# Seven block products for eight in the first 256 features of x @ w_in, from token group 4 on, with shared sums copied inside PSUM

## The chip, the cores and the metric

One core of one Trainium2 chip. The metric is the device time of one execution of the whole program, in microseconds (us). The engines are TensorE (matmuls; PE in the profile, its weight loads PEld), VectorE (DVE), ScalarE (ACT), GpSimd (POOL) and SyncE (SP, here a queue of DMAs).

## What is computed

An mLSTM cell over 4 batches, 8 heads, 768 steps and 40 dimensions per head; its output, as 3072 tokens of 320 features, goes through a two-layer block with a "tanh shrink" between.

```python
for t in range(S):                       # S = 768
    m_new = np.maximum(f_gate[:, :, t] + m, i_gate[:, :, t])
    f_stab, i_stab = np.exp(f_gate[:, :, t] + m - m_new), np.exp(i_gate[:, :, t] - m_new)
    C = f_stab * C + i_stab * einsum('bhd,bhe->bhde', vt, kt)
    n = f_stab * n + i_stab * kt
    y[:, :, t] = sigmoid(o_gate) * einsum(C, qt) / max(|n.qt|, 1)
x = y as [3072, 320]
h = x @ w_in                             # [3072, 2048]
g = h - np.tanh(h)
out = g @ w_out                          # [3072, 320]
```

All products are in f32; TensorE makes two passes (two loads, two matmuls) of each.

## The kernel before

The cell works in 24 units of 128 tokens (`n` in the code). Two units make a token group `g` of 256 tokens, so there are 12. The 2048 hidden features are cut in 8 pairs `p` of two blocks of 128. An *item* is one group with two pairs. Its up products fill two PSUM banks `ph_up` (128 hidden features x 2 pairs x 256 tokens each, one bank for each block of a pair). ScalarE squares them (`z`), with the row sums accumulated, and squares again (`q`); VectorE makes `gt` = c z h (the "cube") and then `gt` = (q + c') gt (the "last" step). That is the polynomial for h - tanh(h).

The down product with `w_out` is made in seven block products for eight (a Strassen-Winograd form). For it VectorE makes sums of `gt` (`s`, `s1` to `s4`) and, once, of `w_out` (`wT`); 14 products of 128x160 an item are accumulated over a whole group in three banks `pS0`, `pS1`, `pS2`, the first two with the tags `po0` and `po1`. After the last item of a group `put_together` copies a part `a` out of `pS0` (ScalarE) and makes the output `ob` from the three banks with four VectorE operations; ScalarE issues its DMA. The next group takes the same banks.

Up to 212 us a planner (a list scheduler with costs and ranks) orders units 0 to 11 and the groups 0 to 3. After that comes the main loop, which this case is about: 32 items, four for each of the groups 4 to 11, here numbered #0 (from 212.09 us) to #31. Iteration x makes the up products of item x and, since `LAG` is 1, the down products of item x-1. `merge` writes out each iteration's TensorE steps in order (the list `dense`) and puts other work between by a clock of estimated costs: `Clock.later(key, wait, step)` holds a step back for a time, and `Clock.need(key)` issues at once whatever a key still holds. Instructions on an engine run in the order in which they are written (the classes `Pinned` and `T` keep it). The cell work of units 12 to 23 is spread over the main loop: an even item has crossed scores `ps` (then `P` on VectorE), an odd one outputs and state (`pT`, `pc`, then `zt`, `yt`, state on VectorE). Items #24 to #31 have little or none. A unit's output `ys` is turned into feature rows through DRAM (`yt`, `y_rows`) and lands in `xT` by SP's DMAs.

An item's up products are eight of 128 features x 256 tokens (two pairs, two blocks, two chunks of 128 input features) and, for the remaining 64 features, eight "quarter" products (`rest`) that run in a quarter of the array each. The main loop's body before is

```python
dense, rest = up(some, shrink(x), bool(scored or new[:1]))
dense.append((..., lambda: halves(rest, *(crossed_scores(n) for n in new[:1]))))
...
dense += down_seven(some)                # of item x-1: all 14 products
```

Of the kernel before, what the change touches and what calls it, by code (L numbers as in the profile page):

```python
# [49 lines left out]
FP = mybir.dt.float32  # L50
# [29 lines left out]
def kernel(  # L80
# [195 lines left out]
    FROM = (0, 128, DM - 128)  # L276
    NK = 2
    HALF = 64
    assert FROM[1] + HALF == FROM[2]
# [41 lines left out]
    w_out = const.tile([128, NFF, DM], FP, name="w_out")  # L321


    xT = [const.tile([128, NK + 1, TG], FP, name=f"xT{i}") for i in range(NX)]

# [24 lines left out]
    def load_unit(n, names=("kz", "qz", "v", "k", "o", "q2"), queue=SP, behind=(), crossed=False):  # L350
        c, b = divmod(n, B)
        t = ld.setdefault(n, {})
        t["crossed"] = crossed
        for name in names:
            if crossed and (name == "v" or name == "k" and n + B < NU):
                whole = load.tile([L, H if name == "v" else WIDE, D], FP, name=name, tag=name, bufs=3)
                t[name] = whole
                if name == "k":
                    G.memset(whole[:, H:], 0.0)
                load_crossed(whole[:, 0:H], (v if name == "v" else k)[b, c])  # L360
            elif name in ("kz", "qz"):
                t[name] = load.tile([128, HH, L], FP, name=name, tag=name, bufs=3)
                for i in range(2):
                    src = kT if name == "kz" else qT
                    dma = queue.dma_start(out=t[name][i * HALF:i * HALF + D], in_=src[b, c, :, i * HH:(i + 1) * HH])
                    if behind:
                        tc.add_manual_dep(dma.ins, behind[-1].ins.name, SYNC, reason="order of transfers")
            elif name == "k":
                if n + B < NU:
                    t["k"] = load.tile([L, WIDE, D], FP, name="k", tag="k", bufs=3)  # L370
                    queue.dma_start(out=t["k"].rearrange("p h d -> p (h d)"),
                                    in_=bass.AP(k.tensor, k[b, c].offset, [[H * D, L], [1, WIDE * D]]))
            elif name != "q2":
                src, bufs = {"v": (v, 3), "o": (o_gate, 4)}[name]
                t[name] = load.tile([L, H, D], FP, name=name, tag=name, bufs=bufs)
                queue.dma_start(out=t[name], in_=src[b, c])
            elif c:
                t["q2"] = load.tile([TOP, len(TRIOS), L], FP, name="q2", tag="q2", bufs=3)
                for i in range(TRIO):
                    queue.dma_start(out=t["q2"][i * D:(i + 1) * D, 0:len(range(i, H, TRIO))], in_=qT[b, c, :, slice(i, H, TRIO)])  # L380
# [50 lines left out]
    NS = NG * NP + 2  # L431
# [160 lines left out]
    def blocks_of(p):  # L592

        def slices(a, n):
            return slice(a * 128, (a + n) * 128)

        every, whole = slice(0, 128), [(slice(0, 128), slices(0, 2), moe_w_in[0:128, slices(2 * p, 2)])]
        odd = moe_w_in[FROM[1]:FROM[1] + 128, slices(2 * p + 1, 1)]
        both = bass.AP(odd.tensor, odd.offset, [[DFF, 128], [(FROM[2] - FROM[1]) * DFF - 128, 2], [1, 128]])
        whole.append((every, slices(2, 2), both))  # L600
        half = (FROM[1], FROM[2] + HALF)
        for i in range(2):
            whole.append((slice(i * HALF, (i + 1) * HALF), slices(4, 1), moe_w_in[half[i]:half[i] + HALF, slices(2 * p + i, 1)]))
# [7 lines left out]
    ys = [const.tile([L, DM], FP, name=f"ys{i}") for i in range(2)]  # L611
# [122 lines left out]
    def gate(n, in_parts=False, den=None):  # L734

        t = un[n]
        ph, sg = t["ph"], t["o"]
        den = den or att.tile([L, H], FP, name="den", tag="den")


        def over():
            V.scalar_tensor_tensor(out=den, in0=ph[:, :, D], scalar=-1.0, in1=inv[:, t["c"], t["hs"]], op0=OP.mult, op1=OP.max)
            V.tensor_tensor(out=den, in0=den, in1=ph[:, :, D], op=OP.max)
            V.reciprocal(out=den, in_=den)

        def shares():
            for h in range(H):
                A.mul(out=sg[:, h], in_=sg[:, h], mul=den[:, h:h + 1])

        def product():  # L750
            y = t["y"] = ys[n % 2]
            V.tensor_tensor(out=y.rearrange("p (h d) -> p h d", d=D), in0=ph[:, :, 0:D], in1=sg, op=OP.mult)
# [32 lines left out]
    def keep_x(n):  # L785
        g, tt = divmod(n, GT)
        A.copy(out=xT[g % NX][:, :, tt * L:(tt + 1) * L], in_=un[n]["px"])

    BLOCK = 32
    NB = (NK + 1) * 128 // BLOCK  # L790

    def turn_by_store(n):
# [7 lines left out]
        V.transpose(flat[:, NK * 128:], y[:, FROM[NK]:])  # L800
        rows = dram.tile([(NK + 1) * 128, L], FP, name="y_rows", tag=f"y_rows{n % 4}")
# [3 lines left out]
        for i in range(2):  # L805
            half = slice(i * HALF, (i + 1) * HALF)
            SP.dma_start(out=xT[g % NX][half, :, tt * L:(tt + 1) * L], in_=rows.rearrange("(c p) t -> p c t", p=128)[half])
# [80 lines left out]
    def gate_turned(n):  # L888
# [18 lines left out]
        def product(a):  # L907
            part = slice(0, BLOCK) if a == 0 else slice(BLOCK, D)
            to, by = (x.rearrange("p (g c) d -> p g c d", c=2)[:, :, :, part] for x in (y.rearrange("p (h d) -> p h d", d=D), sg))
# [31 lines left out]

    def in_seven(g, p):
# [14 lines left out]
    def sums_of_g(some):  # L957
        a = [[gT[some][i][:, :, tt * L:(tt + 1) * L] for i in range(2)] for tt in range(GT)]
        s1, s2, s3 = (conv.tile([128, 2, L], FP, name=name, tag=tag, bufs=2)[:, 0:len(some)]
                      for name, tag in (("s1", "w_e"), ("s2", "w_m"), ("s3", "w_r")))  # L960
        s4 = mlp.tile([128, 2, L], FP, name="s4", tag="s4", bufs=1)[:, 0:len(some)]
# [10 lines left out]
    def down_seven(some):  # L972
# [18 lines left out]
        steps = [(0.0, lambda: Clock.need(some))]  # L991
        final = some[-1] == (NG - 1, NP - 1)
        for k in (0, 1, 5, 3, 4, 2, 6) if final else range(7):
            for x, (_, p) in enumerate(some):
                even, odd = (w_out[:, 2 * p + i, :].rearrange("p (two n) -> p two n", two=2) for i in range(2))
                a11, a12, a21, a22 = (gT[some][i][:, x, tt * L:(tt + 1) * L] for tt in range(GT) for i in range(2))
# [4 lines left out]
                steps.append((0.27, lambda where=where, a=a, x=x, b=b: product(where, a, x, b)))  # L1001
# [82 lines left out]
    def up(some, shrink, quarters=False):  # L1084
# [4 lines left out]
        def product(i, x, j):  # L1089
            g, p = some[x]  # L1090
            f = 2 * p + i
            at = ((0, 2, 1), (0, 1, 2))[i][j]
            if j < NK:
                col = (i, 3 - i)[j]
                lhs, rhs = w_in[:, p, col * 128:(col + 1) * 128], xT[g % NX][:, at, :]
            else:
                rows = slice(i * HALF, (i + 1) * HALF)
                lhs, rhs = w_in[rows, p, 2 * NK * 128:], xT[g % NX][rows, at, :]
            T.matmul(ph[i][:, x, :], lhs, rhs, start=(x == 0 and j == 0), stop=(j == NK), skip_group_check=True)

        def quarter(i, x, c):
            g, p = some[x]
            rows, cols, first = slice(i * HALF, (i + 1) * HALF), slice(c * HALF, (c + 1) * HALF), 2 * NK * 128 + c * HALF
            T.matmul(ph[i][cols, x, :], w_in[rows, p, first:first + HALF], xT[g % NX][rows, ((0, 2, 1), (0, 1, 2))[i][NK], :],
# [9 lines left out]
    def shrink_steps(x, some, ph):  # L1114
# [17 lines left out]
        return square, again, cube, product  # L1132

# [26 lines left out]
    def shrink(x):  # L1160
        def steps(some, ph):
# [5 lines left out]
            for i in range(2):  # L1167
                Clock.later(some, 0.9 + 0.35 * n * i, lambda i=i: cube(i))
                Clock.later(some, 1.0 + 0.75 * n + 0.35 * n * i, lambda i=i: product(i))
# [7 lines left out]
    def down(x, some, g, p, first, last, evict_at_once=True):  # L1177
        def product(i, tt):
# [5 lines left out]
            T.matmul(po[tt], gT[some][i][:, x, tt * L:(tt + 1) * L], w_out[:, f, :], start=start, stop=stop)  # L1184
# [51 lines left out]
    assert 2 * len(items) == NS  # L1236
# [201 lines left out]
    def plan_item(x):  # L1438
# [46 lines left out]
        if seven:  # L1485
# [3 lines left out]
            def begin_run():  # L1489
# [6 lines left out]
                for _, step in steps[:3 * n + 1]:  # L1496
# [4 lines left out]
            for k, (cost, do, need) in enumerate(((0.82 * n, begin_run, [*shrunk, *sums_ready]),  # L1501
                                                  (0.54 * n, lambda: [step() for _, step in steps[3 * n + 1:5 * n + 1]], g),
                                                  (0.54 * n, lambda: [step() for _, step in steps[5 * n + 1:7 * n + 1]], []))):
# [27 lines left out]
    for x in range(START):  # L1531
        plan_item(x)
    busy = []
# [34 lines left out]
    for p in range(SPLIT):  # L1568
        spread_over([(0.0, lambda p=p: [step() for _, step in sums_of_weights(p)])], START + p / 2, START + 0.5 + p / 2)
    banks[:] = [name for name in ("b0", "b1") if name != third["tag"]]  # L1570
# [5 lines left out]
    for x in range(START, len(items) + LAG):  # L1576
        dense, new, scored = [], [], news
        for slot, x0, x1 in begins[x]:
            spread_over(cell_slot(*slot), x0, x1)
            if slot[0] is not None:  # L1580
                new.append(slot[0])
        if x < len(items):
            some = tuple(run[:2] for run in items[x])
            dense, rest = up(some, shrink(x), bool(scored or new[:1]))
# [4 lines left out]
        some = tuple(run[:2] for run in items[x - LAG])  # L1589
        if in_seven(*some[0]):  # L1590
            dense += down_seven(some)
        else:
            for i, run in enumerate(items[x - LAG]):
                dense += down(i, some, *run)
        if x == len(items):
            dense.insert(4, (0.0, count))
            dense.insert(13, (0.0, load_count))
# [107 lines left out]
    with tc.If(loaded[0] > 0):  # L1705
# [17 lines left out]
        for g in range(NG):  # L1723
            for n in range(g * GT, (g + 1) * GT):
# [3 lines left out]
                un[n]["vs_end"] = scaled(n, 1, "vs_end", 1)  # L1728
# [70 lines left out]
```

## Time and profile before

| | us |
|---|---|
| median of 3 runs | 512.26 (511.17 to 514.05) |
| profiled execution: span, from its first instruction to its last | 518.8 |
| TensorE busy in it | 512.1 |
| VectorE busy | 371.7 |
| ScalarE busy | 205.6 |
| GpSimd busy | 40.3 |

The profiled execution has no other time than its span; it lies 6.5 us (1.3%) above the median of the runs without a profile. Times in rows are from the span's start. In a row of the timeline stand the start, the time from the first start to the last end, the engine, the line, the operation, out<-in by the program's names, the shape and the count. Line L106 is that of a helper that records all operations of the other engines, and L129 that of TensorE's, so rows are told apart by their tiles.

### The profile page before, as it was taken

The numbers are of one execution on the slowest core, as the hardware profiler recorded it, in microseconds if no ns is written. First come the engines' busy times: TensorE is split into PE (matmuls) and PEld (weight loads), VectorE is DVE, ScalarE is ACT, GpSimd is POOL, SyncE is SP. The second block draws the span as 40 slices with busy tenths as digits, with TensorE's granted clock in tenths as the row PEclk, the third lists the DMA queues.
The fourth block names the chain that finished last, engine by engine and source line by source line (L and its number), as shares of the span: only waits on it lengthen the run. The fifth ranks groups of instructions, "written<-read, shape, count | busy, mean of one in ns | idle before, by whom it ended". The sixth has DMA issues, their size and how long they took to land.

```text
span 518.8 us, 11220 instructions
## 1 busy us (share of the span) xinstructions
PE 512.1 (99%) x4281; PEld 441.9 (85%) x4281; DVE 371.7 (72%) x840; ACT 205.6 (40%) x523; POOL 40.3 (8%) x88
## 2 busy tenths in 40 slices
PE   9999999999999999999999999999999999999996
PEld 5778878888889888898988988988988989888885
DVE  3589969998865766687785785786776767764634
ACT  3167489476564242423323323323324224231412
POOL 4421414330000000000000000000000000000000
PEclk9999999999999999999999999999999999999999
DMA  7968456554000300005344355344334442320001
GB/s 230 270 183 249 118 174 178 169 106 104 9 1 6 92 27 10 18 27 106 69 109 104 73 121 115 73 115 105 70 104 100 76 116 33 69 57 0 27 2 31
DMA packets 112420, 47.26 MB, mean 91 GB/s; under 512 B 87080, under 2 KB 106088, under 8 KB 112360
## 3 DMA queue, kind: packets, MB, share of 16 engines
q1 hardware_dynamic: 106128, 31.72, 27.3%
q0 software_dynamic: 3040, 10.82, 7.0%
q10 hardware_dynamic: 3192, 3.93, 2.2%
q8 instruction: 36, 0.59, 0.5%
q14 instruction: 24, 0.20, 0.1%
HBM read 36.75 MB, written 9.44 MB: 89 GB/s over the span
## 4 chain that ended last, share of the span: by engine, by line
PE 98%; ACT 1%; DVE 0%; issue 0%
PE ph_up L129 41%; PE pS L129 31%; PE po L129 7%; PE ph L129 5%; PE ps L129 4%; PE awake L129 3%; PE pT L129 3%; PE pc L129 2%; PE px L133 1%; ACT vs L106 0%; PE gate L129 0%; ACT L106 0%; PE gate L133 0%; DVE ob L106 0%; ACT part L106 0%; ACT o L106 0%
## 5 line engine op out<-in xcount | busy, mean ns | idle before, releaser
L129 PE MATMUL ph_up<-xT,w_in 128*128 128x256 f32 (+2 forms) x1344 | 227.0, 386 | 0.0
L129 PEld LDWEIGHTS ph_up<-xT,w_in 128*128 128x128 f32 (+2 forms) x1344 | 171.5, 173 | 37.3 <-issue 15.3
L106 ACT ACTIVATE z<-ph_up 128x512 f32<-128x512 f32 (+1 forms) x98 | 56.9, 584 | 242.0 <-PE ph_up L129 122.2
L106 DVE SCALAR_TENSOR_TENSOR gt<-ph_up,z 128x512 f32<-128x512 f32 (+1 forms) x98 | 63.5, 676 | 67.1 <-ACT z L106 66.8
L129 PE MATMUL pS<-wT,s 128*128 128x160 f32 x480 | 72.0, 299 | 0.0
L129 PEld LDWEIGHTS pS<-wT,s 128*128 128x128 f32 x480 | 67.4, 190 | 0.0
L106 ACT ACTIVATE q<-z,tiny 128x512 f32<-128x512 f32 (+1 forms) x98 | 66.3, 711 | 1.0
L106 DVE SCALAR_TENSOR_TENSOR gt<-q,gt 128x512 f32<-128x512 f32 (+1 forms) x98 | 63.3, 678 | 0.0
L129 PE MATMUL pS<-w_out,gt 128*128 128x160 f32 x320 | 54.3, 312 | 0.0
L129 PEld LDWEIGHTS pS<-w_out,gt 128*128 128x128 f32 x320 | 44.6, 189 | 6.5 <-issue 3.6
L106 DVE TENSOR_TENSOR P<-ps,over 128x384 f32<-128x384 f32 x24 | 12.3, 553 | 36.4 <-PE ps L129 36.4
L129 PE MATMUL po<-w_out,gt 128*128 128x320 f32 x128 | 38.2, 441 | 0.0
L106 DVE TENSOR_TENSOR s<-gt 128x256 f32<-128x256 f32 x80 | 30.3, 420 | 0.0
L129 PEld LDWEIGHTS po<-w_out,gt 128*128 128x128 f32 x128 | 23.1, 190 | 8.5 <-issue 0.3
L129 PEld LDWEIGHTS ph<-vs,P 128*128 128x128 f32 x192 | 27.4, 215 | 1.0 <-issue 0.6
L129 PE MATMUL pS<-wT,gt 128*128 128x160 f32 x160 | 28.3, 299 | 0.0
L129 PE MATMUL pS<-w_out,s 128*128 128x160 f32 x160 | 28.3, 299 | 0.0
L129 PEld LDWEIGHTS ps<-qz,kz 40*64 40x64 f32 (+1 forms) x576 | 25.1, 163 | 3.2 <-DVE vs L106 0.8
L129 PE MATMUL ph<-vs,P 128*128 128x41 f32 x192 | 27.5, 294 | 0.0
L129 PE MATMUL ps<-qz,kz 40*128 40x128 f32 (+2 forms) x576 | 26.1, 267 | 0.0
L129 PEld LDWEIGHTS pS<-wT,gt 128*128 128x128 f32 x160 | 23.9, 190 | 0.0
L129 PEld LDWEIGHTS pS<-w_out,s 128*128 128x128 f32 x160 | 23.9, 190 | 0.0
(114 smaller groups left out, 502.4 us busy)
## 6 DMA issues: line engine op xcount, KB each, us to landing
w<-in_moe_w_out POOLq DMA_DIRECT2D x8, 640.0 KB, 6.2
w<-in_moe_w_in POOLq DMA_DIRECT2D x16, 256.0 KB, 5.2
kz<-in_kT SPq DMA_DIRECT2D x48, 80.0 KB
o<-in_o_gate SPq DMA_DIRECT2D x24, 160.0 KB
qz<-in_qT SPq DMA_DIRECT2D x44, 80.0 KB
out<-ob ACTq DMA_DIRECT2D x11, 320.0 KB
h_rows<-zt SPq DMA_DIRECT2D x48, 64.0 KB
z_in<-h_rows SPq DMA_DIRECT2D x48, 64.0 KB
```

The costliest lines, as they stand in the source:

```text
L106: i = method(*args, **kwargs)
L129: return cls.keep(nc.tensor.matmul(*args, **kwargs))
L133: return cls.keep(nc.tensor.transpose(*args, **kwargs))
```

## The change

For items #0 to #30 the first 256 features (two chunks of 128) by 256 tokens (two units) are treated as 2x2 blocks and multiplied in seven block products of 128x128x128 for eight, for both pairs: 14 matmuls of 128 columns instead of eight of 256. #31 keeps `up`. In a bank X stand `a` and `c` (later overwritten as `d`), in Y `b` and `e`. Sums of x (`s1` to `s4`, `sum_x`, kept in the buffers `xT0` and `xT1`, which show up as `xT_88`, `xT_89`) and of `w_in` (`sum_w_in`, kept in `sums_in` and, for p of 4 and more, in `parts_of`) are made by VectorE. The shared partial sums are passed on in PSUM by ScalarE: stage one makes c and a, then ScalarE copies a to `b` and c to `cs` in SBUF; stage two adds to b, which is copied to `d`; stage three adds to b, which is copied to `e`, and makes the rest. At the end VectorE adds `cs` to d and to e and writes `both`, from which half of the polynomial is made; the other half reads a and b from PSUM.

Between the stages stand six of the 14 down products of item x-1 (three after stage one, three after stage two), the last eight behind the cell pieces. The first four read only the first half of `gt`, so the steps for it are held under the keys `"early"` and `"late"`, and a down product calls for what it reads.

With it go: a new cut of `w_in` in the weight DMAs; `ys` wider by a copy of its last 64 columns (12 units), so that the second `yt` transpose has 64 columns instead of 128; three `xT` DMAs for two; slots for `xT`; `q2` kept in `sums_in`; `sums` with a column more per item.

```diff
-    FROM = (0, 128, DM - 128)
+    FROM = (0, 128, DM - 64)
...
+            V.tensor_copy(out=y[:, DM:], in_=y[:, FROM[NK]:DM])
...
-        V.transpose(flat[:, NK * 128:], y[:, FROM[NK]:])
+        V.transpose(flat[:, NK * 128:], y[:, FROM[NK]:DM])
...
+            if i == 0:
+                SP.dma_start(out=to, in_=bass.AP(rows.tensor, rows.offset, [[L, HALF], [128 * L, NK + 1], [1, L]]))
+            else:
+                SP.dma_start(out=to[:, 0:NK], in_=rows[0:NK * 128].rearrange("(c p) t -> p c t", p=128)[half])
+                SP.dma_start(out=to[:, NK], in_=rows[FROM[NK]:])
...
-        steps = [(0.0, lambda: Clock.need(some))]
+        steps = []
...
+                keys = [(some, "early"), (some, "late"), some][:1 if k < 2 else 2 if k == 2 else 3]
+                steps.append((0.27, lambda ...: [*map(Clock.need, keys), product(where, a, x, b)]))
...
+    def sum_x(g):
+        (b11, b12), (b21, b22) = x_of(g)
+        s1, s2, s3, s4 = (sums_x_of(g)[:, i] for i in range(4))
+        V.tensor_tensor(out=s3, in0=b11, in1=b12, op=OP.subtract)
+        V.tensor_tensor(out=s1, in0=b12, in1=b22, op=OP.add)
+        V.tensor_tensor(out=s2, in0=s1, in1=b11, op=OP.subtract)
+        V.tensor_tensor(out=s4, in0=b21, in1=s2, op=OP.subtract)
+
+    def up_in_seven(x, some):
+        banks_of = X, Y = [ps_h.tile([128, 2, n, L], FP, name="ph_up", tag=f"ph{i}") for i in range(2)]
+        a, c, d, b, e = X[:, 0], X[:, 1], X[:, 1], Y[:, 0], Y[:, 1]
+        cs = mlp.tile([128, n, L], FP, name="cs", tag="s4", bufs=1)
...
+        one = then(product(c, t(2), s3, True) + product(a, w(0), b11), copy(b, a), copy(cs, c))
+        two = then(product(b, t(1), s2), copy(d, b))
+        three = then(product(b, t(0), s1), copy(e, b)) + product(a, w(2), b21) + product(d, t(3), b22) + product(b, w(3), s4)
+        rest = [lambda i=i, k=k, j=j: quarter(i, k, j) for k in range(n) for j in range(2) for i in range(2)]
...
+            square_b = square(z[0][:, 1], b, 0)
+            add_d = V.tensor_tensor(out=both[:, 0], in0=d, in1=cs, op=OP.add)
+            after(square(z[0][:, 0], a, 1), add_d)
+            after(V.tensor_tensor(out=both[:, 1], in0=e, in1=cs, op=OP.add), square_b)
+            again(0)
+            square(z[1], both, 2)
+            again(1)
+            Clock.later(early, 1.0, lambda: cube(gt[0][:, 1], b, z[0][:, 1]))
+            Clock.later(early, 1.1, lambda: cube(gt[0][:, 0], a, z[0][:, 0]))
+            Clock.later(early, 1.9, lambda: last(0))
+            Clock.later(late, 2.6, lambda: cube(gt[1], both, z[1]))
+            Clock.later(late, 3.3, lambda: last(1))
+            Clock.later(some, 3.4, lambda: sums_of_g(some))
...
+        downs = down_seven(some)
...
+                stages, rest = up_in_seven(x, some)
+                dense = stages[0] + downs[0:3] + stages[1] + downs[3:6] + stages[2]
+                downs = downs[6:]
...
+        dense += downs
```

On TensorE, an item with `pT` (an odd one) that follows a group's end stands before as this; `pS_2735` to `pS_2737` are the three banks of the new group:

```order
L129 MATMUL ph_up<-xT_91,w_in 128x256 x8
L129 MATMUL ph_up<-xT_91,w_in 64x256 x8
L129 MATMUL pT<-qz,state_0_150 64x128 x8
L129 MATMUL pT<-P,vs 64x128 x4
L129 MATMUL pT<-P,vs 64x64 x4
L129 MATMUL pT<-P,vs 64x128 x4
L129 MATMUL pT<-P,vs 64x64 x4
L129 MATMUL pc<-vs,k 64x41 x8
L129 MATMUL pS_2735<-w_out,gt 128x160 x4
L129 MATMUL pS_2737<-wT,gt 128x160 x2
```

Now such an item starts as follows (`xT_88` holds the sums of x, `xT_90` is x, `pS_3783` to `pS_3785` are the new group's banks; the first row is the last product of the old group):

```order
L129 MATMUL pS_3271<-w_out,s 128x160 x2
L129 MATMUL ph_up<-xT_88,sums_in 128x128 x2
L129 MATMUL ph_up<-xT_90,w_in 128x128 x2
L129 MATMUL pS_3783<-w_out,gt 128x160 x3
L129 MATMUL ph_up<-xT_88,sums_in 128x128 x2
L129 MATMUL pS_3783<-w_out,gt 128x160
L129 MATMUL pS_3785<-wT,gt 128x160 x2
L129 MATMUL ph_up<-xT_88,sums_in 128x128 x2
L129 MATMUL ph_up<-xT_90,w_in 128x128 x2
L129 MATMUL ph_up<-xT_90,sums_in 128x128 x2
L129 MATMUL ph_up<-xT_88,w_in 128x128 x2
L129 MATMUL ph_up<-xT_90,w_in 64x2x128 x8
```

The first product of the new group's banks has moved from behind the eight up products, the rest and the cell pieces to right behind stage one, four 128-column products after the old group's last.

VectorE at a group's end before, from the cubes of the group's next item on (`gt_3509`, `gt_3510`) to the output `ob_3547`:

```order
L106 SCALAR_TENSOR_TENSOR gt_3509<-ph_up_3469,z_3505 128x512
L106 SCALAR_TENSOR_TENSOR gt_3510<-ph_up_3470,z_3506 128x512
L106 SCALAR_TENSOR_TENSOR gt_3509<-q_3507,gt_3509 128x512
L106 SCALAR_TENSOR_TENSOR gt_3510<-q_3508,gt_3510 128x512
L106 TENSOR_TENSOR s3_3538<-gt_3509 128x256
L106 TENSOR_TENSOR s1_3536<-gt_3509,gt_3510 128x256
L106 TENSOR_TENSOR s2_3537<-s1_3536,gt_3509 128x256
L106 TENSOR_TENSOR s4_3539<-gt_3510,s2_3537 128x256
L106 TENSOR_TENSOR ob_3547<-pS0_3187,a_3548 128x2x160
L106 TENSOR_TENSOR u_3549<-pS1_3188,ob_3547 128x320
L106 TENSOR_TENSOR ob_3547<-pS1_3188,u_3549 128x160
L106 TENSOR_TENSOR ob_3547<-pS2_3189,u_3549 128x320
```

and now (`gt_3228` is the half from a and b, `gt_3229` that from `both`):

```order
L106 TENSOR_TENSOR both_3223<-ph_up_3166,cs_3168 128x256
L106 TENSOR_TENSOR both_3223<-ph_up_3167,cs_3168 128x256
L106 TENSOR_TENSOR P_3165<-ps_3197,over_140 128x384
L106 TENSOR_TENSOR P_3165<-ps_3198,over_140 128x384
L106 SCALAR_TENSOR_TENSOR gt_3228<-ph_up_3167,z_3224 128x256
L106 SCALAR_TENSOR_TENSOR gt_3228<-ph_up_3166,z_3224 128x256
L106 SCALAR_TENSOR_TENSOR gt_3228<-q_3226,gt_3228 128x512
L106 SCALAR_TENSOR_TENSOR gt_3229<-both_3223,z_3225 128x512
L106 TENSOR_TENSOR ob_3250<-pS0_2755,a_3251 128x2x160
L106 TENSOR_TENSOR u_3252<-pS1_2756,ob_3250 128x320
L106 TENSOR_TENSOR ob_3250<-pS1_2756,u_3252 128x160
L106 TENSOR_TENSOR ob_3250<-pS2_2757,u_3252 128x320
```

The four `ob` steps have moved from behind the last step and the sums of `gt` to between the cube and the last step of its second half, `gt_3229`.

On ScalarE the same place now reads (the copies between `ph_up` are a to b, b to d and b to e of the next item):

```order
L106 ACTIVATE z_3224,sums_134<-ph_up_3167 128x256
L106 ACTIVATE z_3224,sums_134<-ph_up_3166 128x256
L106 ACTIVATE q_3226<-z_3224,tiny_120 128x512
L106 ACTIVATE z_3225,sums_134<-both_3223 128x512
L106 ACTIVATE q_3227<-z_3225,tiny_120 128x512
L106 COPY a_3251<-pS0_2755 128x160
L106 COPY ph_up_3255<-ph_up_3254 128x256
L106 COPY cs_3256<-ph_up_3254 128x256
L106 COPY ph_up_3254<-ph_up_3255 128x256
L106 DMA out<-ob_3250 128x2x320
L106 COPY ph_up_3255<-ph_up_3255 128x256
```

Before, four operations of 512 columns (two `z`, two `q`) were all that an item had here beside the copy `a` and the output DMA; the three copies in PSUM and `cs` have come in.

More of the change, by code (lines that the diff above doesn't have):

```diff
@@ L1183, in product @@
             Clock.need(some)
-            T.matmul(po[tt], gT[some][i][:, x, tt * L:(tt + 1) * L], w_out[:, f, :], start=start, stop=stop)
+            T.matmul(po[tt], blocks(some)[tt][i][:, x], w_out[:, f, :], start=start, stop=stop)
             if stop and evict_at_once:
@@ L1727 @@
                 prepare(n)
[L1728 removed]
+                un[n]["vs_end"] = scaled(n, 1, "yt", 1)
                 un[n]["column"]()
```

145 lines of the change are left out of this document (103 added, 42 removed).

## The prediction

> **What bounds the kernel now.** I read the page first (busy shares, granted clock, chain of waits), then busy time by window for single items, then the timeline of each engine inside them.
>
> ```profile
> span 518.8 us, 11220 instructions
> PE 512.1 (99%) x4281; PEld 441.9 (85%) x4281; DVE 371.7 (72%) x840; ACT 205.6 (40%) x523; POOL 40.3 (8%) x88
> PEclk9999999999999999999999999999999999999999
> PE 98%; ACT 1%; DVE 0%; issue 0%
> ```
>
> TensorE is the chain, at full granted clock. The next view gives busy time per engine for whole main-loop items (columns: window, length, then PE, PEld, DVE, ACT, POOL, clock, DMA share, GB/s). Scores and state alternate, so I call items with `ps` S and those with `pT` T.
>
> ```profile
> 298.56:308.75 10.19, 10.19 (x127) 9.13 (x126) 9.16 (x26) 2.91 (x7) 0.44 (x4) 1.00 0.63 144
> 308.75:317.89 9.14, 9.14 (x94) 8.13 (x93) 5.71 (x13) 2.95 (x8) 0.00 (x0) 1.00 0.42 79
> 317.89:328.08 10.19, 10.19 (x127) 9.13 (x126) 7.56 (x22) 2.91 (x7) 0.12 (x1) 1.00 0.46 107
> 458.71:467.23 8.52, 8.52 (x55) 7.45 (x53) 4.02 (x9) 2.49 (x6) 0.00 (x0) 1.00 0.10 26
> ```
>
> TensorE is busy for the whole of every item: a pass saved is time saved, a wait added is time lost. VectorE, at 5.71 to 9.16 us, has the least room of the others. Inside an item the order is up products, cell pieces, 14 down products:
>
> ```profile
> 299.43 2.75 PE L129 MATMUL ph_up<-xT,w_in 128*128 128x256 f32 x12
> 308.75 4.64 PE L129 MATMUL ph_up<-xT,w_in 128*128 128x256 f32 x32
> 313.21 0.85 PE L129 MATMUL ps<-qz,kz 40*64 40x128 f32 x32
> 315.72 1.79 PE L129 MATMUL pS<-wT,s 128*128 128x160 f32 x12
> L129 PE MATMUL pS<-wT,s 128*128 128x160 f32 x480 | 72.0, 299 | 0.0
> L129 PE MATMUL ph_up<-xT,w_in 128*128 128x256 f32 x768 | 176.4, 380 | 0.0
> L129 PEld LDWEIGHTS ph_up<-xT,w_in 128*128 128x128 f32 x768 | 142.7, 190 | 17.9
> 155.50 0.75 PEld L129 LDWEIGHTS ph<-vs,P 128*128 128x128 f32 x6
> ```
>
> Every product is two passes. A 256-column pass takes (2.75-.38)/11 = .2155 us; a 160-column one (1.79-.30)/11 = .1355, so a down product .271 and 14 of them 3.80.
>
> **Gain on TensorE.** In 31 items (#0 to #30) eight products of 256 columns (16 passes, 3.45 us) become 14 of 128 (28 passes). Where six 128-wide loads stand back to back they follow each other by (.75-.19)/5 = .112, though each lasts .19, so loads overlap and the pass sets the pace: .112 at most, and half of .2155 = .108 at least. I take .111, near the measured end: 28 x .111 = 3.11, a gain of .34 per item, **10.5 us** in all (9.7 to 13.1). The third 64 features keep their eight quarter products.
>
> A page of the Trainium skill speaks against this: "TensorE: Matmul & The Clock Gate", Part 3, says that a weight load overlaps a running matmul only where its row group differs. By it each pass here would cost its load too; the loads above, .19 long at a distance of .112, disagree.
>
> **The PSUM copies.** Three of the four copies of 256 columns per item (b from a, d from b, e from b; `cs` goes to SBUF) stand between TensorE stages, each with three down products (.816) or `a`,`d`,`b` products behind it as cover. No row shows a PSUM-to-PSUM copy; the nearest are
>
> ```profile
> L106 ACT COPY a<-pS 128x160 f32<-128x160 f32 x12 | 3.5, 293 | 14.6 <-PE pS L129 14.6
> L106 ACT COPY xT<-px 128x384 f32<-128x384 f32 x12 | 5.6, 480 | 13.8 <-PE px L133 13.8
> 63.83 0.82 PE L133 MATMUL px<-ident,ys 128*128 128x128 f32 x6
> 64.36 0.86 ACT L106 COPY xT<-px 128x384 f32<-128x384 f32 x2 [2.88 <-PE px L133]
> ```
>
> Between 293 and 480 ns lies .37 for 256 columns. The copy began .20 after the slot of its third pass (63.83+3x.11); with .05 back to TensorE it takes .20+.37+.05 = .62, at the long end .73, under .816: hidden, cost 0. If the cover were gone it would cost .6 twice an item. The decision lies at a copy of .56.
>
> The page "ScalarE: Activation LUTs" of the Trainium skill has ScalarE nearer to PSUM than to SBUF as destination; that would shorten the copy and leave the sum as it is; no row here shows it.
>
> **VectorE and ScalarE.** Per item VectorE gains two adds (`both`), and one cube is split in two of 256; per group `sum_x` adds four, per later pair `sum_w_in` three. POOL still issues four DMAs a weight pair (two halves of another cut), before the span's first third is over; SP issues three `xT` DMAs in place of two for each of 12 units, and its later loads queue behind the third. The chain above holds no DMA and the units are loaded items ahead, so cost 0; if that cover went, TensorE would wait at the first `ph_up` of a group. In the first 212 us VectorE gets a 64-column copy for each of 12 units and `sum_w_in` for four pairs, some 24 short operations (nearest row: .24 for 64 columns, .42 for 256), beside a TensorE whose own order there stays; taken as 0, and 1 us either way for what a planner shifts. On the other side the wide `yt` transposes only 64 instead of 128 columns in its second part. What matters is when `gt` is ready, since six downs of item x-1 now stand *between* the up stages of item x. Prices:
>
> ```profile
> 303.31 0.60 ACT L106 ACTIVATE z<-ph_up 128x512 f32<-128x512 f32 x1 [4.80 <-PE ph_up L129]
> 303.81 0.20 ACT L106 ACTIVATION_READ_ACCUMULATOR z<-ph_up 128x1 f32 x1
> 304.47 1.33 ACT L106 ACTIVATE q<-z,tiny 128x512 f32<-128x512 f32 x2
> 305.70 0.53 ACT L106 COPY zt<-pT 128x448 f32<-128x448 f32 x1
> 304.04 1.29 DVE L106 SCALAR_TENSOR_TENSOR gt<-ph_up,z 128x512 f32<-128x512 f32 x2 [0.58 <-ACT z L106]
> 305.49 0.64 DVE L106 STREAM_TRANSPOSE yt<-ys 128x256 f32<-128x256 f32 x2
> 306.62 0.24 DVE L106 STREAM_TRANSPOSE zt<-pT 128x64 f32<-128x64 f32 x1
> 308.48 0.68 DVE L106 SCALAR_TENSOR_TENSOR gt<-q,gt 128x512 f32<-128x512 f32 x1
> 314.12 1.02 DVE L106 TENSOR_TENSOR P<-ps,over 128x384 f32<-128x384 f32 x2 [3.29 <-PE ps L129]
> 35.49 0.38 ACT L106 ACTIVATE z<-ph_up 128x256 f32<-128x256 f32 x1 [1.01 <-PE ph_up L129]
> 35.77 0.19 ACT L106 ACTIVATION_READ_ACCUMULATOR z<-ph_up 128x1 f32 x1
> 36.00 0.42 DVE L106 SCALAR_TENSOR_TENSOR gt<-ph_up,z 128x256 f32<-128x256 f32 x1
> ```
>
> E is the modelled end of an item's last `ph_up` matmul (308.75+4.64; the square of the T item begins .11 after 298.56+4.64). ScalarE: square of `b` .11, square of `a` .55 (a new wait: for the first add, .08 to .50; behind it in ScalarE's queue stand all the later ones, so both `gt` shift with it), `q` 1.06 to 1.78, square of `both` 1.67 with its read done at 2.48, second `q` 2.52, then a copy at 3.13. VectorE in a T item: adds .08 and .61 (the second waits for the first square; `yt`, `P` and the cubes queue behind it), `yt` .95, cubes 1.48 and 1.82, last of `gt0` 2.27, third cube 2.87, `zt` transpose 3.47, `zt` add 3.71 (it waits for the .53 copy), wide transpose 4.27, state 1.86 us after the first `zt` (306.62 to 308.48), `gt1` done 6.09. TensorE after E: cell pieces 10.19-4.64-3.80 = 1.75, eight downs 2.17, stage one .89 (to 4.81), d0 to d2 (5.62), stage two (6.07), d3 (6.34), and d4 is the first that reads `gt1`: .2 to spare. The twelve T items wait for nothing, but the six with `sum_x` by a little over .1: **0.7**.
>
> S items: cell pieces .70, so stage one ends at 3.76; `gt0`, behind `P`, is ready at 3.4, `gt1` at 4.7 and needed at 5.29. No wait, unless the item ends a group. Then `put_together` stands on VectorE between the third cube and the last of `gt1`, with these prices (and, in item #0, `wT` and the add of `part`):
>
> ```profile
> 218.48 0.32 DVE L106 TENSOR_TENSOR wT<-w_out 128x160 f32<-128x160 f32 x1
> 219.54 1.28 DVE L106 SCALAR_TENSOR_TENSOR gt<-ph_up,z 128x512 f32<-128x512 f32 x2
> 224.67 0.49 DVE L106 TENSOR_TENSOR ob<-pS,a 128x320 f32<-128x320 f32 x1
> 225.19 0.49 DVE L106 TENSOR_TENSOR u<-pS,ob 128x320 f32<-128x320 f32 x1
> 225.71 0.72 DVE L106 TENSOR_TENSOR ob<-pS,u 128x160 f32<-128x160 f32 x2
> 226.47 0.83 DVE L106 TENSOR_TENSOR ob<-ob,part 128x640 f32<-128x640 f32 x1
> 263.33 0.38 ACTq L106 DMA_DIRECT2D out<-ob  x1
> ```
>
> In such an item (#4, 8, 12, 16, 20) the first `ob` runs 3.88 to 4.37, and d0 of the new group needs the bank `po0` that it reads: free at 4.42, wanted at 3.76, wait .66. Behind the waiting product all of TensorE's queue is pushed, and with it ScalarE's copy to `d`, which then finds its engine free; d4 now wants `gt1` at 5.95, but that stands behind 1.7 of `ob` work and ends at 6.26: wait .36. **1.0 each, 5.1** for five. The output DMA, issued by ScalarE between its copies to `d` and to `e`, takes .38 from about 6.3 on and is through before the copy to `e` is wanted, at 7.4: 0. Before, 14 downs and eight up products lay between, so none of this showed. Item #0: four `wT` (218.48 to 219.54) ahead and the `part` add (.83) behind make 1.73 and 1.21, **2.9**, and .15 in #1. #28, with no cell pieces, wants d0 at 3.14 and, since the copy of `a` starts only at 3.13, gets 4.0: .88 and .35, **1.2**. #24 is like it with the late denominators in front of the last of `gt1`: 1.2 to 2.9, **2.1**. Together 12.1.
>
> **Sum.** 512.3 - 10.5 + 12.1 = **513.8**. The profiled span, 518.8, is 6.5 above the median of the runs; the rows are of that execution, and I carry the 1.3% as an offset, since both items of the sum are differences.
>
> **Rivals.**
> - *The waits at group ends don't bind* (faster). If VectorE's `ob` work comes earlier than I walked it, by .7 the first wait is gone. Speaks for it: my start-to-start times are stacked over eight instructions, .08 each would do. With none of the waits 512.3-10.5 = 501.8; with half 507.8.
> - *VectorE becomes the bound* (slower): T's slack is .2, its busy share would go from (9.16+7.56+2x5.71)/38.66 = 73% of a group of four items to 32/37.3 = 86%: more per item are two adds of .335 (start to start; it lies between .30, half of the .60 from one 512-wide to the next at 304.04, and the .42 that a 256-wide one lasts) and .07 for the cube cut in two, .74 x 4 = 3.0, and .8 for `sum_x` a group, 3.8 in all. If the chain up to `gt1` is .5 longer, twelve items lose .3 more each: 517.4. It decides from .2 on.
> - *The copies outlast their cover* (slower): if copy and hand-over take .15 longer than .816 in 62 places, 9 more: about 522. Against it: .62 by rows.
> - *Loads are not hidden*, by the rule above: then 28 passes take .19 and not .111, 28 x .079 x 31 = 69 more, 583. The row of loads speaks against it.
>
> **How the numbers follow.** No change is within 2.6 us of 512.3 (0.5%, what a measurement of this kernel can tell). Forecast .39 (509.7 to 514.8); waits that don't bind .25, all of it faster; VectorE the bound .22; copies .12; loads .02. So faster .25, same .39, slower .36. The range leaves out the loads, most of the copies and the low end of the waits: 505.5 to 520; the forecast alone would have 510 to 515.
>
> **What would show it.** Right: `ph_up` at 128 columns at .108 to .112 a pass; the largest idle gaps of TensorE at the first new `pS` product in #4 to #20, .6 to .7 long, put down to `ob`, and a second in front of the first `gt1` product; copies of .3 to .48. Wrong: gaps in every item in front of `ph_up` (copies), in every T item in front of d4 (VectorE), passes over .112, or no gap at group ends.

## The result, and the profile after

The changed kernel is slower: 1.0116 of before (95% interval 1.0068 to 1.0164), 518.2 us for 512.3, and in a second measurement 1.0129 (1.0107 to 1.0150). The median over all its first runs is 522.16, because executions of either kernel fall into two groups 8 to 10 us apart, and the ratio compares the faster groups. The forecast was 513.8 with 505.5 to 520: the time is inside the range and on the expected side, but not "within 0.5%", the case that the forecast called the likeliest.

The page of the changed kernel:

```profile
span 516.2 us, 12435 instructions
...
PE 497.5 (96%) x4709; PEld 442.5 (86%) x4709; DVE 417.3 (81%) x1001; ACT 262.0 (51%) x709; POOL 40.8 (8%) x88
...
PE 77%; DVE 14%; ACT 3%; DMA 2%; issue 2%; SPq 1%; DVEq 0%; ACTq 0%
```

The chain was TensorE alone (98%); now VectorE has 14% of it. The span is *shorter* than that of before (518.8) though the kernel is slower. In the profile of before TensorE made its first 27 us at about half pace, as the same 16 `ps` matmuls show (first row before, second after), and its main loop began 8.7 us later (212.09 and 203.42):

```profile
11.23 2.08 PE L129 MATMUL ps<-qz,kz 40*128 40x128 f32 x16
```

```profile
8.96 1.16 PE L129 MATMUL ps<-qz,kz 40*128 40x128 f32 x16
...
203.42 0.61 PE L129 MATMUL ph_up<-xT,sums_in 128*128 128x128 f32 x4
```

The half pace and not the change is behind this: the profile of the run called e8 below, a version of the changed kernel, began at half pace too, and its main loop starts at 212.31. That of the run without cover also began so. The traces are therefore compared from item #0 on: 306.74 before (212.09 to 518.83), 516.22 - 203.42 = 312.80 after, 6.1 more, as the runs say. Now the waits of TensorE over the main loop (total, times, longest):

```profile
PE pS L129 <- DVE ob L106: 5.9, 8, 1.6
PE pS L129 <- DVE gt L106: 5.0, 10, 1.4
PE ph_up L129 <- DVE gt L106: 0.2, 1, 0.2
```

Ahead of `<-` stand the matmuls that waited, behind it the engine and the tile that they waited for. No wait of TensorE is for a copy or a DMA. Now single items by window, each from the start of the last `ph_up` matmul of one item to that of the next. From here on #n is the window that ends with the last `ph_up` of #n. What the forecast places in #4, the work behind that item's up products, so lies in the window of #5. First before (T, S, and #9, the S at a group's end), then after (T, S, the same #9, and #12, a T behind `sum_x`):

```profile
264.17:274.35 10.18, 10.18 (x131) 9.12 (x127) 7.14 (x18) 2.91 (x7) 0.21 (x2) 1.00 0.33 80
274.35:283.50 9.15, 9.15 (x100) 8.14 (x96) 6.80 (x16) 2.95 (x8) 0.00 (x0) 1.00 0.58 121
293.68:302.83 9.15, 9.15 (x100) 8.14 (x95) 7.73 (x19) 3.24 (x9) 0.00 (x0) 1.00 0.48 92
```

```profile
260.04:269.89 9.85, 9.85 (x143) 9.36 (x139) 7.67 (x19) 5.22 (x15) 0.21 (x2) 1.00 0.43 92
269.89:278.73 8.84, 8.84 (x112) 8.40 (x108) 7.75 (x21) 4.32 (x12) 0.00 (x0) 1.00 0.46 105
288.58:298.67 10.09, 9.34 (x112) 8.50 (x108) 9.06 (x23) 4.50 (x13) 0.00 (x0) 1.00 0.50 119
317.36:328.29 10.93, 10.12 (x144) 9.40 (x139) 9.33 (x26) 5.27 (x15) 0.12 (x1) 1.00 0.44 97
```

An undisturbed item gains .33 (10.18 to 9.85) or .31 (9.15 to 8.84), and .37 in the last ones, which have no cell pieces (8.52 to 8.15). Before, a group's end costs nothing (9.15 in both S rows). The third row after shows something else: the item is 1.25 longer than its undisturbed sister (10.09 - 8.84), but TensorE is idle for only .75 of it (10.09 - 9.34). So I count a wait by the length of its item, and not by its gap. The same place on TensorE (d0 to d2 are the six matmuls at 293.48, d3 the two at 294.85, d4 and d5 the four at 295.45):

```profile
292.29 0.61 PE L129 MATMUL ph_up<-xT,w_in 128*128 128x128 f32 x4
293.48 1.08 PE L129 MATMUL pS<-w_out,gt 128*128 128x160 f32 x6 [0.58 <-DVE ob L106]
294.40 0.61 PE L129 MATMUL ph_up<-xT,sums_in 128*128 128x128 f32 x4
294.85 0.44 PE L129 MATMUL pS<-w_out,gt 128*128 128x160 f32 x2
295.45 0.78 PE L129 MATMUL pS<-wT,gt 128*128 128x160 f32 x4 [0.17 <-DVE gt L106]
```

and on VectorE, from the adds to `gt1`:

```profile
289.07 0.96 DVE L106 TENSOR_TENSOR both<-ph_up,cs 128x256 f32<-128x256 f32 x2 [1.71 <-PE ph_up L129]
289.96 1.01 DVE L106 TENSOR_TENSOR P<-ps,over 128x384 f32<-128x384 f32 x2
290.88 0.74 DVE L106 SCALAR_TENSOR_TENSOR gt<-ph_up,z 128x256 f32<-128x256 f32 x2
291.73 0.69 DVE L106 SCALAR_TENSOR_TENSOR gt<-q,gt 128x512 f32<-128x512 f32 x1
292.34 0.69 DVE L106 SCALAR_TENSOR_TENSOR gt<-both,z 128x512 f32<-128x512 f32 x1
292.94 0.48 DVE L106 TENSOR_TENSOR ob<-pS,a 128x320 f32<-128x320 f32 x1
293.46 0.49 DVE L106 TENSOR_TENSOR u<-pS,ob 128x320 f32<-128x320 f32 x1
293.99 0.72 DVE L106 TENSOR_TENSOR ob<-pS,u 128x160 f32<-128x160 f32 x2
294.63 0.68 DVE L106 SCALAR_TENSOR_TENSOR gt<-q,gt 128x512 f32<-128x512 f32 x1
```

d0 begins when the first `ob` leaves `pS0` (293.43), d4 when the last step of `gt1`, behind the three other `ob` steps, is done (295.31): the two waits of the forecast, at their places.

The waits of the whole main loop, predicted, by the gap shown, and by the length of the item against undisturbed ones. The places have the forecast's numbers, except in the last row; their windows are those of #5, 9, 13, 17, 21, of #1, #3, #25 and #29, and in the last row #12, #16 and #20:

| place | predicted | gaps | longer by |
|---|---|---|---|
| ends of five groups (#4, 8, 12, 16, 20) | 5.1 | 3.75 | 6.27 |
| #0, with `wT` and `part` | 2.9 | 2.67 | 3.18 |
| weight sums in #1, #2 | .15 | .18 | .40 |
| #24 | 2.1 | 2.11 | 2.61 |
| #28 | 1.2 | .84 | 1.34 |
| T items behind `sum_x` | .7 | 1.49 | 2.25 |
| sum | 12.1 | 11.0 | 16.05 |

With 31 x .33 = 10.2 gained and .3 in the tail this gives 16.05 - 10.2 + .3 = 6.1, the whole difference.

### The profile page after: what moved, and what is told of

It is laid out like the page before. It is cut to its first block, busy times and chain, and to the rows that moved or that the text cites. A ratio compares the mean times of both kernels' runs of the same rounds, so it can differ in the third digit from the quotient of the medians.

```text
span 516.2 us, 12435 instructions
## 1 busy us (share of the span) xinstructions
PE 497.5 (96%) x4709; PEld 442.5 (86%) x4709; DVE 417.3 (81%) x1001; ACT 262.0 (51%) x709; POOL 40.8 (8%) x88
## 4 chain that ended last, share of the span: by engine, by line
PE 77%; DVE 14%; ACT 3%; DMA 2%; issue 2%; SPq 1%; DVEq 0%; ACTq 0%
PE ph_up L129 34%; PE pS L129 23%; PE po L129 7%; DVE gt L106 4%; PE ph L129 4%; PE ps L129 3%; PE pc L129 2%; PE pT L129 2%; DVE ob L106 2%; ACT z L106 2%; PE awake L129 2%; DVE P L106 1%; SPq L106 1%; PE px L133 1%; DMA z_in<-h_rows 1%
## 5 line engine op out<-in xcount | busy, mean ns | idle before, releaser
L129 PE MATMUL ph_up<-xT,w_in 64*64 64x256 f32 (+3 forms) x1276 | 171.2, 356 | 0.0
L129 PEld LDWEIGHTS ph_up<-xT,w_in 128*128 128x128 f32 (+2 forms) x1276 | 126.9, 168 | 19.9 <-issue 4.8
L106 ACT ACTIVATE z<-ph_up 128x256 f32<-128x256 f32 (+1 forms) x98 | 44.1, 450 | 111.3 <-PE ph_up L129 108.9
L106 ACT COPY ph_up<-ph_up 128x256 f32<-128x256 f32 x93 | 33.2, 357 | 85.7 <-PE ph_up L129 57.5
L106 DVE SCALAR_TENSOR_TENSOR gt<-ph_up,z 128x256 f32<-128x256 f32 (+1 forms) x98 | 46.3, 499 | 21.5 <-ACT z L106 21.3
L106 DVE TENSOR_TENSOR both<-ph_up,cs 128x256 f32<-128x256 f32 x62 | 26.1, 423 | 39.8 <-PE ph_up L129 36.7
L129 PE MATMUL ph_up<-xT,sums_in 128*128 128x128 f32 x256 | 39.1, 275 | 0.0
L129 PE MATMUL ph_up<-xT,part 128*128 128x128 f32 x240 | 36.7, 275 | 0.2 <-DVE gt L106 0.2
L129 PEld LDWEIGHTS ph_up<-xT,sums_in 128*128 128x128 f32 x256 | 34.7, 191 | 0.0
L129 PEld LDWEIGHTS ph_up<-xT,part 128*128 128x128 f32 x240 | 32.5, 191 | 0.4 <-issue 0.4
```

The source lines that it names most:

```text
L106: i = method(*args, **kwargs)
L129: return cls.keep(nc.tensor.matmul(*args, **kwargs))
```

## Experiments

Theory A: the passes gain .33 in every item, and waits at a few places, counted by item lengths, take more than that. Rival B: copies and a fuller VectorE burden all items, and a wait taken away comes back elsewhere.

**Plain up products where a group's downs begin.**

```diff
-            if x < len(items) - 1:
+            if x < len(items) - 1 and (x - START) % 4 != 1:
```

> Edit: the eight iterations in which a new group's down products begin (#1, #5, ... #29) go back to the plain up products (eight of 256 columns, all downs behind); the other 23 items stay as changed. Theory A (the loss sits at the group starts: d0 waits for the bank that ob reads, d4 for gt1 behind ob; about 13.4 us in the trace of the changed kernel when each wait is counted by the length of its item and not by its gap alone): the waits go, 8 x .33 = 2.6 of gain is given back, so about 518.2 - 13.4 + 2.6 = 507.4, faster than before by about 1%. Rival B (copies and a fuller VectorE burden all items and the waits only move to other places): no more than a quarter of that is won, 515 or above.

Measured 0.9983 (0.9953 to 1.0013), 510.6 beside 511.6: no difference from before that is clear of noise, and between the two theories. The waits at all group ends are gone, as A says. But 3.2 us of the expected gain are missing, in the trace 5.2. Above all, #2 is 2.2 too long (VectorE has the sums of weights there), #12 2.9 and so 1.9 more than in the changed kernel (`sum_x` and the denominators), #26 is .7 too long, and five other items .2 each, to which the runs e7 and e8 come back. There B is right, at the group ends A.

**No cover for the copies.**

```diff
-                dense = stages[0] + downs[0:3] + stages[1] + downs[3:6] + stages[2]
-                downs = downs[6:]
+                dense = stages[0] + stages[1] + stages[2]
```

> Edit: the six down products between the up stages go behind the cell pieces, so nothing covers the PSUM copies. Theory A: each of the two hand-overs a to b and b to d costs its whole way, .20 to the copy, .36 copy, .05 back = .61, and by the gap in the trace a little less: 62 x .61 = 38 us; the waits for ob and gt1 vanish from the trace; 512.3 - 10.4 + 38 = 540. Rival B (a copy in PSUM is mostly hidden by the pipeline anyway): no more than .36 each, 524 or below. If a hand-over takes .25 beyond its gap, as the waits of the changed kernel do, about 548.

Measured 1.0693 (1.0632 to 1.0753), 547.8: the third figure of the expectation, and neither A's 540 nor B's 524. The trace, TensorE and then ScalarE:

```profile
301.09 0.61 PE L129 MATMUL ph_up<-xT,w_in 128*128 128x128 f32 x4
302.15 0.71 PE L129 MATMUL ph_up<-xT,sums_in 128*128 128x128 f32 x4 [0.45 <-ACT ph_up L106]
303.35 0.71 PE L129 MATMUL ph_up<-xT,sums_in 128*128 128x128 f32 x4 [0.49 <-ACT ph_up L106]
```

```profile
301.74 0.36 ACT L106 COPY ph_up<-ph_up 128x256 f32<-128x256 f32 x1 [3.04 <-PE ph_up L129]
...
302.94 0.36 ACT L106 COPY ph_up<-ph_up 128x256 f32<-128x256 f32 x1 [0.56 <-ACT cs L106]
```

Stage one's slots end at 301.09 + 4 x .111 = 301.53; copy at 301.74, TensorE at 302.15: .62 on the way, the .62 of the forecast. Its four passes then take .71 and not .61. With this .10 a hand-over costs .72; items are 1.45 longer, twice that. All items lose it alike (two of them .28 more) and no group end shows: what made the difference between items was the downs between the stages.

**`sum_x` earlier.**

```diff
-        spread_over([(0.0, lambda g=g: sum_x(g))], item(g * NP) - 0.7, item(g * NP) - 0.5)
+        spread_over([(0.0, lambda g=g: sum_x(g))], item(g * NP) - 0.95, item(g * NP) - 0.85)
```

> Edit: only sum_x of each later group stands earlier in VectorE's queue, at the begin of the item ahead of the group instead of its middle, ahead of the operations that wait for z_in. Theory A (in #12 and #16 the four sums stand between the late z_in and the adds and push gt1 by 1.1 to 1.6): the items #12, #16 and #20 lose 1.08, .95 and .22 less, 516.0 in place of 518.2. Rival B (the late z_in alone is enough): within 0.5 of 518.2.

A miss: 1.0173 (1.0114 to 1.0232). #12, #16 and #20 do lose less (by .69, .95 and .22), but seven other items (#3, #7 and on to #27) are .55 longer each, since `sum_x` now stands ahead of the last step of `gt1`, for which d4 waits. VectorE has too little slack for 1.1 us at a place that is merely early.

**Cell pieces as cover.**

```diff
...
+            if x < len(items) - 1 and not (first and not scored):
...
+                if first:
+                    dense, downs, turned = stages[0] + turned + stages[1] + downs[0:3] + stages[2], downs[3:], []
...
```

Here `turned` holds the cell pieces `pT` and `pc`.

> Edit: in the six iterations with a group's first downs and cell pieces (#1, #5, ... #21) the cover of the first copy is pT and pc, that of the second d0 to d2, and the other eleven downs stand behind; #25 and #29, which have no cell pieces, go back to the plain up products. Theory A: d0 comes 2 us later than ob has left its bank and d4 far behind gt1, so the waits of 13.4 us go and only 2 x .33 of gain is given back: 518.2 - 13.4 + .7 = 505.5, 1.3% faster than before, unless the earlier pT brings a wait for P of its own (.3 to .6 each, 507.5 to 509). Rival B: 514 or above.

A miss: 1.0054 (1.0020 to 1.0089), by the ratios 3.2 us less than the changed kernel, in place of 12.7. d0 and d4 wait no more, but other things came in their place. In #1 stage three waits 1.33 for ScalarE's copy to `d`: it stands in ScalarE's queue behind the output DMA, which waits for `ob`. In #2 stage one waits 1.01. The pair #5 and #6 takes 19.78, against 18.69 undisturbed; .61 of this is a new wait (gap .36) of the next stage one for cubes that still read its bank. The other .48 shows no gap, but can be read from the rows:

```profile
256.17 0.71 PE L129 MATMUL ph_up<-xT,sums_in 128*128 128x128 f32 x4
260.43 0.54 PE L129 MATMUL pS<-w_out,gt 128*128 128x160 f32 x2
264.05 0.68 PE L129 MATMUL ph_up<-xT,part 128*128 128x128 f32 x4 [0.36 <-DVE gt L106]
```

The first two stand behind cell and quarter pieces, and are .10 longer than the same rows elsewhere (.61 and .44). With the other changes between products of the full array and smaller pieces, .05 to .11 each, and less one such place that #6 no longer has, that makes .35. The last .13 is in #6, where the rows of d0 to d2 and of stage two are .04 and .09 longer. Why a change of shape costs this is not shown.

**The changed kernel once more, and `sum_x` where VectorE is idle.** In front of the wait in #12 VectorE stood idle for `z_in` and then did everything at once:

```profile
315.05 0.42 DVE L106 TENSOR_TENSOR s<-gt,s 128x256 f32<-128x256 f32 x1
316.49 0.17 DVE L106 SCALAR_TENSOR_TENSOR den<-z_in,inv 128x8 f32<-128x8 f32 x1 [1.02 <-DMA z_in<-h_rows]
...
317.55 0.49 DVE L106 TENSOR_TENSOR xT<-xT 128x128 f32<-128x128 f32 x2
318.07 0.62 DVE L106 TENSOR_TENSOR xT<-xT,xT 128x128 f32<-128x128 f32 x2
...
319.08 0.75 DVE L106 TENSOR_TENSOR both<-ph_up,cs 128x256 f32<-128x256 f32 x2
```

The item's last `ph_up` matmul began at 317.36 and ended, by the profile, at 317.73; the first add, .08 after that end in the forecast, came 1.35 after it.

```diff
+        spread_over([(0.0, lambda g=g: sum_x(g))], item(g * NP) - 0.87, item(g * NP) - 0.77)
```

> The changed kernel itself, beside the next two on the same chip. Both theories: 1.012 of before, with the same waits at the same places.

> Edit: only sum_x of each later group stands between the sums of gt and the denominators that wait for z_in, where VectorE is idle (from 315.5 to 316.5 in the trace of the changed kernel). Theory A': sum_x costs by what it stands in front of; neither gt1 (as in the early version, .55 in each of seven items) nor the adds (as in the changed kernel, 1.08, .95 and .22 in #12, #16 and #20) is behind it here, so 2.2 less than the changed kernel. Rival B': VectorE has no room of 1.1 anywhere, so it is lost somewhere again: 0 to .5 less.

Measured 1.0129 (1.0107 to 1.0150) and 1.0104 (1.0089 to 1.0118): the intervals overlap, and the medians of the runs on which the ratios rest are 518.7 and 516.7, 1.9 us less where 2.2 were expected. The items are clear. #12 goes from 11.34 to 9.95, #16 from 10.69 to 9.95, #20 from 9.48 to 9.34; #25 gets .25 longer and #4 and #24 .1 each. So `sum_x` costs by what stands behind it in the queue, not by its length.

**The places put together.**

```diff
-            if x < len(items) - 1:
+            if x < len(items) - 1 and (x - START) % 4 != 1 and x - START not in (2, 3):
...
```

with `sum_x` as in the last run and `sum_w_in` from #3 on. This is run e7.

> Edit: plain up products in the eight iterations with a group's first downs and in #2 and #3 (ten in all, so 21 items in seven products), sum_x as in the run before, sum_w_in of the later pairs spread over the items from #3 on instead of #1 and #2. Theory A: 21 x .33 = 7.0 gained; the waits that were left in the run with eight plain items (#2 2.2, #12 2.9, and .2 in each of #16, #20, #24) go; what is left is .4 in #26 and .3 in the tail: 511.7 - 7.0 + 1 to 2 = 505.7 to 507, 1% faster than before. Rival B (waits only move): 510 to 512.

Measured 0.9932 (0.9916 to 0.9948), which makes 508.2 of the 511.7 that the expectation starts from: faster than before, by 1.2 to 2.5 us less than expected. A single kind of gap is left on TensorE:

```profile
PE ph_up L129 <- DVE gt L106: 0.5, 2, 0.3
```

The two items with these gaps, #5 and #26, are .41 and .97 longer than their sisters. And #6, #10, #14, #18 and #22 are .19 longer than their passes, without a gap. The next run, e8, takes that up:

```diff
-                Clock.later((some, "early"), 1.0 + 0.75 * n + 0.35 * n * i, lambda i=i: product(i))
+                Clock.later((some, "early"), 1.0 + 0.75 * n + 0.05 * n * i, lambda i=i: product(i))
```

> Edit to the run e7 alone: in the ten plain items the last step of gt1 is due earlier, so that it stands ahead of the zt and state operations on VectorE. Theory A (every wait counts, those under .25 that show no gap too): in #6, #10, #14, #18 and #22 of e7 the item is .19 longer than its passes, since d2 waits for that gt1; it goes, about 1 us less than e7, 0.991 of before. Rival B (item lengths without a gap are noise of the trace): as e7, 0.993.

Measured 0.9912 (0.9879 to 0.9944), the lowest ratio of all versions. Its interval overlaps that of e7, so the runs do not tell A from B; the items do. #10 in e7 and in e8, with d0 to d2 in it:

```profile
293.03:304.71 11.68, 11.68 (x156) 11.03 (x151) 9.01 (x24) 4.75 (x13) 0.44 (x4) 1.00 0.41 101
...
299.84 1.17 PE L129 MATMUL pS<-w_out,gt 128*128 128x160 f32 x6
```

```profile
301.99:313.47 11.48, 11.48 (x155) 10.99 (x151) 9.02 (x24) 4.75 (x13) 0.44 (x4) 1.00 0.41 103
...
308.80 0.98 PE L129 MATMUL pS<-w_out,gt 128*128 128x160 f32 x6
```

The .20 is gone in all five items (11.48 in #6, #10 and #14, 10.89 in #18 and #22). In e7 `gt1` was done at 300.42, inside the six matmuls, and in e8 ahead of them. Neither version has a gap there, so a wait of .2 is not seen in TensorE's busy time.

**One `ob` step instead of four.**

```diff
...
+            if g < FIRST:
+                V.tensor_tensor(out=u, in0=bank[1], in1=twice(ob[:, 4]), op=OP.add)
...
+            else:
+                G.memset(ob[:, 1:4], 0.0)
```

> Edit to the changed kernel: for groups 4 to 10 only the first of the four ob operations (the one that reads pS0) is left in, the other three are left out and a fill by GpSimd stands for them, so the output is not the whole sum. Theory A (two separate waits: d0 for the bank, d4 for gt1 queued behind the rest of ob): the gap of .58 in front of d0 stays in #5, #9, #13, #17, #21, the .17 in front of d4 goes with its .25, in #29 too, and #25 loses some 1.2 less: 3.7 less than the changed kernel, 1.005 of before. Rival B (one lateness that d0 and d4 only share out): the first gap grows by what the second loses, 1.011 to 1.013.

Measured 1.0085 (1.0055 to 1.0116), by the ratios 1.6 us less than the changed kernel in place of A's 3.7; the interval just misses A's 1.005 and holds B's 1.011. So the time does not decide for A, but the rows do. At a group's end:

```profile
294.49 0.61 PE L129 MATMUL ph_up<-xT,w_in 128*128 128x128 f32 x4
295.68 1.08 PE L129 MATMUL pS<-w_out,gt 128*128 128x160 f32 x6 [0.58 <-DVE ob L106]
...
297.32 0.71 PE L129 MATMUL pS<-wT,gt 128*128 128x160 f32 x4
```

The gap before d0 is the same .58, that before d4 is gone, and the item has 9.68 in place of 10.09. These are two separate waits, of .85 and .41, as A says. But #25 was no shorter (11.05 in place of 10.76), which is most of what is missing from A's figure: the long wait there is not behind `ob`. VectorE's denominators, which wait for the DMA `z_in`, are in front of that `gt1`; its gap ran from 1.3 to 2.1 over the traces that have it.

## Why the prediction was right, and where its sizes were off

The path was right: nearly the same gain in every item, and waits at the places that the forecast names. The sum was 4 us too low, and the time is inside the range because the range was wide. It lies close to the 517.4 of the rival "VectorE becomes the bound", but that is chance: the T items, from which that figure comes, did not get .3 longer.

- **Pass pace and gain: right.** 128-column passes were forecast at .111, .34 an item:

```profile
L129 PE MATMUL ph_up<-xT,sums_in 128*128 128x128 f32 x256 | 39.1, 275 | 0.0
...
L129 PEld LDWEIGHTS ph_up<-xT,sums_in 128*128 128x128 f32 x256 | 34.7, 191 | 0.0
```

  A stage of four passes takes .61, so (.61 - .275)/3 = .11. The measured gain is .31 to .37. The loads of .191 are hidden in passes of .11, and the rival "loads are not hidden" fell with this. The Trainium skill, "TensorE: Matmul & The Clock Gate", Part 3, says that a load overlaps only where the row group differs. This trace does not agree: all these loads fill the whole array, and they follow each other every .11.
- **Copies hidden: right.** No wait for them in the changed kernel, .62 on the way when uncovered. The copy was put at .37; the trace has

```profile
L106 ACT COPY ph_up<-ph_up 128x256 f32<-128x256 f32 x93 | 33.2, 357 | 85.7 <-PE ph_up L129 57.5 <-ACT cs L106 14.5 <-issue 13.3
...
L106 ACT COPY cs<-ph_up 128x256 f32<-128x256 f32 x31 | 11.8, 379 | 0.0
```

  The Trainium skill, "ScalarE: Activation LUTs", section "Step-by-step: what each stage is for", has PSUM as the quicker destination for ScalarE. This trace agrees: 357 ns into PSUM and 379 into SBUF for the same 256 columns.
- **Group ends: the right waits, and a term left out.** The forecast reckons in slots, from one possible start of a pass to the next: .66 for d0 and .36 for d4. In slots the trace has .75 (the slots of stage one end at 292.29 + 4 x .111 = 292.73, d0 starts at 293.48) and .33 (295.12 to 295.45). The gaps .58 and .17 are shorter, since they count from the modelled end of the last pass. But the waits cost .85 and .41. The step that failed is "wait .66", "wait .36", "1.0 each": it took the time by which the reader is late for the whole cost, and left out that the first row behind a wait is .10 or .07 longer (1.08 for .98, .78 for .71). Five group ends cost 6.27 in place of 5.1.
- **`sum_x` in T items, .7: wrong, and the largest miss of the sum.** It cost 2.25, in three items in place of six. "A little over .1" took `sum_x` for done ahead of E; in #12 and #16 it stood behind denominators that were waiting for a DMA (in #12 `z_in`, 1.02), and the adds behind it. The forecast put the DMAs of SP's queue at "cost 0", because TensorE's chain held none. It overlooked that they hold up VectorE: before, that cost TensorE next to nothing (VectorE waited 1.9 us for `z_in` in all, now 1.7), but now TensorE waits for what VectorE makes next. That the third `xT` DMA makes them later is not shown.
- **#0, #24, #28:** 6.2 forecast, 7.1 measured, with gaps of 5.6.
- **Rivals.** "The waits don't bind" and "the copies outlast their cover" fell. "VectorE becomes the bound" is half true: no T item waits by itself, the slack of .2 holds (9.85, no gap), but 1.1 us more in one place, late or early, is a wait of TensorE.

## What to carry to other kernels

Where an engine has no idle time, work that is moved between its steps has to be ready earlier; look for every reader that moves forward, for what stands ahead of its producer in another queue, and for the bank or buffer that its first write takes over. Price a wait by the length of the stretch against an undisturbed one, since the gap shows only part of it. A saving that is the same everywhere (.33 here) can be kept by leaving the change out at the few places where the waits are: 21 items of 31, with the sums moved as well, gave 0.991, where 31 had given 1.012.

## What the runs showed of the hardware

- A wait of TensorE cost about .25 more than its gap (.27 at d0, .24 at d4). A pass of 128 columns lasts .275 in the trace while the next one can start after .111, so .164 of every wait lies under the modelled end of the last pass. And the first row behind the wait is longer: six passes behind a wait took 1.08 (293.48), six without one .98 (first row below). That is .10 more, and .164 + .10 = .26. The load of the first pass starts only when the wait ends (second row), so no earlier pass hides it; that this is the .10 is my reading, which no run isolates. With cell pieces as cover the same .10 stands behind cell and quarter pieces, where no wait is shown.

```profile
204.31 0.98 PE L129 MATMUL pS<-w_out,gt 128*128 128x160 f32 x6
293.48 0.84 PEld L129 LDWEIGHTS pS<-w_out,gt 128*128 128x128 f32 x6 [0.77 <-DVE ob L106]
```

- At the start of the program TensorE ran at about half pace until 27 us in one execution and until about 8 us in another, with the same instructions, while the slices of the granted clock show full speed in both. The versions e7 and e8 have the same instructions in the same order on every engine up to the main loop, and yet it begins at 203.16 in the one profile and at 212.31 in the other:

```profile
203.16 0.61 PE L129 MATMUL ph_up<-xT,sums_in 128*128 128x128 f32 x4
212.31 0.61 PE L129 MATMUL ph_up<-xT,sums_in 128*128 128x128 f32 x4
```

  Two profiled spans can so differ by 9 us for no reason in the kernels.
